# Moving the second batch's transposes and copies ahead of the convolution loop in a fused attention, routed-expert and gated-convolution kernel

## The chip, the core and the metric

The kernel runs on one core of a Trainium2 chip. The metric is the device time of one execution in microseconds (us); lower is better. The engines named below are PE (TensorE: matrix products; PEld is its weight load), DVE (VectorE), ACT (ScalarE), POOL (GpSimd) and SP (SyncE, which here issues DMAs). Each has its own list of instructions, in the order of the program, and semaphores tie the lists together.

## What is computed

The program chains three layers: an attention with cluster masks, a layer of routed experts, and a gated causal convolution. Only the third is touched here (B = 2 batches, S = 768 rows, D = 512 channels, 5 taps):

```
def _moe2_ref(x, w_val, conv_w, w_out):
    B, S, D = x.shape
    K = conv_w.shape[0]
    xp = np.concatenate([np.zeros((B, K - 1, D)), x], axis=1)
    gate_pre = np.zeros((B, S, D))
    for k in range(K):
        gate_pre += conv_w[k][None, None, :] * xp[:, k:k + S, :]
    gate = 1.0 / (1.0 + np.exp(-gate_pre))
    val = x @ w_val
    return gate * val @ w_out
```

## The kernel before

The last stage starts when the experts' output `x2d` is in DRAM. Both products are made to almost full float32 accuracy by splitting each operand into a high part (float32r) and the rest: `xh` and `xl` for x, `vh` and `vl` for w_val, `gh` and `gl` for the gated values, `oh_` and `ol` for w_out. A product is then high x high, low weight x high, and high weight x rest.

**Loads.** SP issues five loads of `x2d` into `xnat` (12 tiles of 128 rows: tile 0, tiles 1-2, 3-5, 6-8 and 9-11; L1075 to L1078). Between the fourth and the fifth it issues the two 1 MB loads of the output weights (L1080, through L293 and L294).

**Transposes.** `x2_tiles(b, t0, n, eng)` takes n tiles of batch b. PE transposes each into a PSUM tile `x2p` (4 transposes of 128x128 a tile, L1102). ACT rounds it into `xh` (L1106), `eng` copies it, unrounded, into `xf` (L1107); after every third tile DVE forms that half of `xl` = `xf` - `xh` (L1111, two instructions). Batch 1's six tiles all go through the two PSUM buffers of the pool `ps_x`, so a transpose of tile t waits until both copies of tile t-2 are done. For batch 0 the copies to `xf` are on DVE, and three of its tiles use the pool `ps_g`; for batch 1 they are on ACT.

**Channels.** A batch has four blocks d of 128 channels, and `order` lists the eight (b, d). For each, `conv0` (ACT, first tap), `conv_a` (DVE, a tap per instruction) and `conv_b` (ACT, the sigmoid) make the gate in `gt`; `value` makes 24 matmuls of 384 columns into a PSUM tile `vp` of the pool `ps_g` (three buffers): `value_hi` 8 for each half c of the rows, then `value_lo` 4 for each half. `value_out` copies `vp` to `vs` on ACT, which frees the buffer; `gated` multiplies on DVE and rounds on ACT into `gh`; `gated_rest` forms `gl` on DVE. `project(b, t)` makes 12 matmuls of 512 columns for one tile of the output, copies it on ACT and stores it.

**Order.** It is written out by hand: nothing moves instructions afterwards. Batch 0's tiles come first, then the value products of (0, 0) and (0, 1), then a loop over n = 1 to 7, in which each step does parts of the gate of `order[n]`, finishes `order[n - 1]`, copies out earlier value products (`evict`), and issues matmuls for later ones (`after[n]`: `value(0, 2)` at n = 1, `value(0, 3)` at n = 2, `value(1, 0)` and `value(1, 1)` at n = 3, `value(1, 2)`, `value(1, 3)` and the projections after). Batch 1's tiles are taken in pairs in steps 1, 2 and 3:

```
        for m in evict.get(n, ()):
            value_out(*order[m])
        if n < 4:
            x2_tiles(1, 2 * n - 2, 2, nc.scalar.copy)
        if n < 7:
            conv0(*order[n + 1])
        gated(*order[n - 1])
```

Of the kernel before, what the change touches and what calls it, by code (L numbers as in the profile page):

```python
# [8 lines left out]
F32 = mybir.dt.float32  # L9
# [4 lines left out]
ALU = mybir.AluOpType  # L14
# [18 lines left out]
def routed_attention_moe_kernel(  # L33
# [12 lines left out]
    nc = tc.nc  # L46
# [703 lines left out]
    for i in range(NI):  # L750
        g, qb, t, h = items[i]
# [334 lines left out]
    xh, xl, xf, gh, gl = ({} for _ in range(5))  # L1086

    def x2_tiles(b, t0, n, eng):
        if t0 == 0:
            xf[b] = ft.tile([128, 4, S + 4], F32, tag=f"xf{b}", name="xf")  # L1090
            nc.gpsimd.memset(xf[b][:, :, 0:4], 0.0)
            xh[b] = fx.tile([128, 4, S], F32R, tag="xh", name="xh")
            xl[b] = fx.tile([128, 4, S], F32R, tag="xl", name="xl")
        xps = []
        for t in range(t0, t0 + n):
            if b == 0 and 2 <= t < 5:
                xps.append(ps_g.tile([128, 2, 512], F32, tag="v", name="x2p")[:, 0, :].rearrange("p (d c) -> p d c", d=4))
            else:
                xps.append(ps_x.tile([128, 4, 128], F32, tag="x", name="x2p"))
        for i in range(n):  # L1100
            for d in range(4):
                nc.tensor.transpose(xps[i][:, d, :], xnat[:, 6 * b + t0 + i, 128 * d:128 * d + 128], ident)  # L1102
        for i in range(n):
            t = t0 + i
            ts = slice(128 * t, 128 * t + 128)
            nc.scalar.copy(xh[b][:, :, ts], xps[i])  # L1106
            eng(xf[b][:, :, 4 + 128 * t:132 + 128 * t], xps[i])  # L1107
            if t % 3 == 2:
                c0 = 128 * t - 256
                for d in range(0, 4, 2):  # L1110
                    nc.vector.tensor_tensor(  # L1111
                        xl[b][:, d:d + 2, c0:c0 + 384], xf[b][:, d:d + 2, 4 + c0:388 + c0],
                        xh[b][:, d:d + 2, c0:c0 + 384].bitcast(F32), op=ALU.subtract,
                    )

    G = {}

    def conv0(b, d):
        G[b, d] = fl.tile([128, S], F32, tag="gt", name="gt", bufs=3)
        nc.scalar.activation(G[b, d], xf[b][:, d, 0:S], AF.Copy, scale=convw_sb[:, d, 0:1])  # L1120

    def conv_a(b, d, ks):
        for k in ks:
            nc.vector.scalar_tensor_tensor(  # L1124
                G[b, d], xf[b][:, d, k:k + S], convw_sb[:, d, k:k + 1], G[b, d], op0=ALU.mult, op1=ALU.add
            )

    def conv_b(b, d):
        nc.scalar.activation(G[b, d], G[b, d], AF.Sigmoid)  # L1129
# [3 lines left out]
    def value_hi(b, d, c):  # L1133
        ds_, cs_ = slice(128 * d, 128 * d + 128), slice(384 * c, 384 * c + 384)
        if c == 0:
            V[b, d] = ps_g.tile([128, 2, 512], F32, tag="v", name="vp")
        for k in range(4):
            nc.tensor.matmul(V[b, d][:, c, :384], vh[:, k, ds_], xh[b][:, k, cs_], start=(k == 0), stop=False)  # L1138
            nc.tensor.matmul(V[b, d][:, c, :384], vl[:, k, ds_], xh[b][:, k, cs_], start=False, stop=False)  # L1139

    def value_lo(b, d, c):
        ds_, cs_ = slice(128 * d, 128 * d + 128), slice(384 * c, 384 * c + 384)
        for k in range(4):
            nc.tensor.matmul(V[b, d][:, c, :384], vh[:, k, ds_], xl[b][:, k, cs_], start=False, stop=(k == 3))  # L1144
# [6 lines left out]
    def value_out(b, d):  # L1151
        VS[b, d] = fl.tile([128, S], F32, tag="vs", name="vs", bufs=3)
        nc.scalar.copy(VS[b, d].rearrange("p (a c) -> p a c", a=2), V.pop((b, d))[:, :, :384])  # L1153

    def gated(b, d):
        if d == 0:
            gh[b] = fx.tile([128, 4, S], F32R, tag="xh", name="gh")
            gl[b] = fx.tile([128, 4, S], F32R, tag="xl", name="gl")
        gt = G.pop((b, d))
        nc.vector.tensor_tensor(gt, gt, VS.pop((b, d)), op=ALU.mult)  # L1160
        nc.scalar.copy(gh[b][:, d, :], gt)
        GT[b, d] = gt

    def gated_rest(b, d):
        nc.vector.tensor_tensor(  # L1165
            gl[b][:, d, :], GT.pop((b, d)), gh[b][:, d, :].bitcast(F32), op=ALU.subtract
        )
# [30 lines left out]
    for t in range(6):  # L1198
        x2_tiles(0, t, 1, nc.vector.tensor_copy)
# [11 lines left out]
    conv0(0, 0)  # L1211
    conv_a(0, 0, (1, 2, 3, 4))
    conv0(0, 1)
    for f in (value_hi, value_lo):
        for c in range(2):
            for d in range(2):
                f(0, d, c)
    for n in range(1, 8):
        conv_a(*order[n], (1, 2))
        conv_b(*order[n - 1])  # L1220
        for m in evict.get(n, ()):
            value_out(*order[m])
        if n < 4:
            x2_tiles(1, 2 * n - 2, 2, nc.scalar.copy)
        if n < 7:
            conv0(*order[n + 1])
        gated(*order[n - 1])
        conv_a(*order[n], (3,))
        gated_rest(*order[n - 1])
        conv_a(*order[n], (4,))  # L1230
        for f in after[n]:
            f()
# [56 lines left out]
```

## Time and profile before

| | us |
|---|---|
| median of 3 runs | 581.74 |
| lowest and highest of them | 581.27, 582.97 |
| the profiled execution, its own time | 581.82 |
| span of the profiled execution | 580.1 |
| last stage, from the first load issued to the end | 488.25 to 580.1 |

All times of rows are counted from the start of the span of one profiled execution. A timeline row gives start and duration of an instruction, or of several of one kind merged (x8), and in brackets how long the engine had been idle before it and what ended that. Matmuls overlap in the pipeline, so the step from one start to the next is what one costs, not its duration. PEclk is the clock granted to TensorE, 1.00 for 2.4 GHz and 0.50 for 1.2 GHz.

### The profile page before, as it was taken

What the parts mean: (1) busy time and instruction counts of PE and PEld (TensorE: products, weight loads), DVE (VectorE), ACT (ScalarE), POOL (GpSimd) and SP (SyncE); (2) the same over time, 40 slices, a digit from 0 to 9 for tenths busy, and PEclk for the clock granted to TensorE, in tenths of its full rate; (3) what the DMA queues carried; (4) which work ended last, traced back from release to release, by engine and by line L of the source; (5) the groups of instructions that cost most, each with busy time, mean ns of one, the idle gap of its engine ahead of it and who ended that gap; (6) DMA issues with size and microseconds to landing.
All of it is one profiled execution on the core that took longest, in us unless ns stands there. A gap on an engine that the chain in (4) does not pass through costs nothing. (4 is left out here: it accounts for less than half of the span.)

```text
span 580.1 us, 9383 instructions
## 1 busy us (share of the span) xinstructions
PE 550.8 (95%) x3485; PEld 442.6 (76%) x3485; DVE 386.5 (67%) x661; ACT 338.7 (58%) x611; POOL 114.6 (20%) x105
## 2 busy tenths in 40 slices
PE   7889999999999999997899999999999998978996
PEld 3756777776767776775788989989989884878885
DVE  5675767575878866467268769678687370887940
ACT  3676777777777686751255655656555352466532
POOL 4001010101030210303530440522504432000000
PEclk9899999999999999997999999999999999997999
DMA  6977777673747464102658778678678775700012
GB/s 147 267 170 237 153 245 157 206 157 96 164 144 156 159 137 141 40 35 105 217 181 311 238 255 297 217 281 282 218 279 281 290 262 188 294 0 2 36 73 108
DMA packets 33103, 104.82 MB, mean 181 GB/s; under 512 B 5713, under 2 KB 6225, under 8 KB 27936
## 3 DMA queue, kind: packets, MB, share of 16 engines
q1 hardware_dynamic: 28816, 97.31, 54.3%
q0 software_dynamic: 3280, 6.32, 2.9%
q8 instruction: 28, 0.46, 0.3%
q10 hardware_dynamic: 960, 0.58, 0.3%
q14 instruction: 19, 0.16, 0.1%
HBM read 63.45 MB, written 24.95 MB: 152 GB/s over the span
## 5 line engine op out<-in xcount | busy, mean ns | idle before, releaser
L620 DVE TENSOR_REDUCE mx<-s 128x1 f32<-128x768 f32 x96 | 91.6, 955 | 60.0 <-PE s L613 53.9
L321 DVE TENSOR_TENSOR wlo<-wraw,whi 128x1024 fp32r<-128x1024 f32 x66 | 89.9, 1364 | 22.8 <-ACT whi L320 22.3
L649 ACT COPY pt<-tp 128x384 f32<-128x384 f32 x148 | 66.0, 487 | 53.8 <-PE tp L644 53.7
L629 ACT ACTIVATE pexp<-s,mx 128x768 f32<-128x768 f32 x96 | 87.5, 912 | 7.6 <-DVE mx L620 5.5
L320 ACT CAST whi<-wraw 128x1024 fp32r<-128x1024 f32 x68 | 70.2, 1045 | 30.7 <-DMA wraw<-in_wq_dram 30.6
L644 PE MATMUL tp<-ident,pexp 128*128 128x128 f32 x576 | 81.4, 277 | 0.6 <-DVE pt L647 0.4
L644 PEld LDWEIGHTS tp<-ident,pexp 128*128 128x128 f32 x576 | 68.2, 142 | 8.2 <-ACT pt L649 3.4
L656 PE MATMUL pv<-pt,vt 128*64 128x384 f32 x360 | 67.8, 498 | 0.2 <-ACT ut L665 0.2
L609 PE MATMUL s<-st 128*128 128x384 f32 x188 | 57.3, 386 | 1.5 <-ACT pexp L629 1.5
L987 PE MATMUL yp<-whi,hhi 128*128 128x512 f32 x136 | 53.8, 395 | 0.0
L991 PE MATMUL yp<-whi,hlo 128*128 128x512 f32 x136 | 53.7, 395 | 0.0
L990 PE MATMUL yp<-wlo,hhi 128*128 128x512 f32 x136 | 53.7, 395 | 0.0
L613 PE MATMUL s<-st 80*128 80x384 f32 x188 | 49.1, 342 | 2.4 <-DMA st<-ohr 2.4
L964 ACT ACTIVATE hhi<-hps 128x512 fp32r<-128x512 f32 (+1 forms) x36 | 20.7, 576 | 51.4 <-PE hps L960 41.6
L965 DVE SCALAR_TENSOR_TENSOR hlo<-hps,hhi 128x512 fp32r<-128x512 f32 (+1 forms) x36 | 23.6, 656 | 31.0 <-ACT hhi L964 25.3
L960 PE MATMUL hps<-xhi,whi 128*128 128x256 f32 x256 | 41.9, 284 | 1.6 <-issue 0.9
L609 PEld LDWEIGHTS s<-st 128*128 128x128 f32 x188 | 28.6, 191 | 18.0 <-ACT pt L649 6.8
L960 PE MATMUL hps<-xlo,whi 128*128 128x256 f32 x256 | 41.2, 280 | 0.6 <-issue 0.4
L960 PE MATMUL hps<-xhi,wlo 128*128 128x256 f32 x256 | 40.7, 279 | 0.0
L656 PEld LDWEIGHTS pv<-pt,vt 128*64 128x64 f32 x360 | 21.9, 136 | 24.1 <-issue 23.7
L339 POOL TENSOR_TENSOR xx<-xkq,xx 128x768 fp32r<-128x768 f32 x8 | 14.6, 1822 | 120.8 <-ACT xx L333 102.6
L238 POOL TENSOR_TENSOR wspace<-wspace 128x512 f32<-128x512 f32 x8 | 14.2, 1781 | 120.8 <-ACT wspace L234 110.3
(225 smaller groups left out, 983.6 us busy)
## 6 DMA issues: line engine op xcount, KB each, us to landing
wraw<-in_wq_dram SPq DMA_DIRECT2D x34, 1024.0 KB, 5.1
st<-xx SPq DMA_DIRECT2D x48, 384.0 KB, 6.8
xkq<-in_kq_dram SPq DMA_DIRECT2D x15, 384.0 KB, 4.4
xslots<-padrow SPq DMA_DIRECT2D x8, 514.0 KB, 7.8
wspace<-in_wd_dram SPq DMA_DIRECT2D x8, 512.0 KB, 5.3
xs<-xslots SPq DMA_DIRECT2D x7, 514.0 KB, 5.8
vt<-in_v_dram SPq DMA_DIRECT2D x8, 384.0 KB, 3.4
out_dram<-os SPq DMA_DIRECT2D x11, 256.0 KB, 2.0
```

Of the source, the lines that this page charges most:

```text
L320: nc.scalar.copy(hi[:, c], t[:, c])
L321: (lo_eng or nc.vector).tensor_tensor(lo[:, c], t[:, c], hi[:, c].bitcast(F32), op=ALU.subtract)
L609: nc.tensor.matmul(ps[:, n, :384], st[:, 1, q0:q0 + 128], st[:, 0, 384 * n:384 * n + 384], start=True, stop=False)
L620: nc.vector.tensor_reduce(mx, ps[:, :, :384], axis=AX.XY, op=ALU.max, negate=True)
L629: nc.scalar.activation(pt, ps[:, :, :384], AF.Exp, bias=mx[:, 0:1], accum_out=Zt[i // 6][:, t, h:h + 1])
L644: nc.tensor.transpose(tp[:, k, :], p[:, 128 * kt:128 * kt + 128], ident)
L649: nc.scalar.copy(dst, tp)
L656: nc.tensor.matmul(PVs[u][64 * h:64 * h + 64, :], Vt[g][:, kt, h, :], PT[u, h][:, kt, :], start=(kt == 0), stop=(kt == NQT - 1), skip_grou ...
L960: nc.tensor.matmul(hp[:, fi, :w], a[:, d, fs], c[:, d, :w], start=(n + d == 0), stop=(n + d == 5))
L987: nc.tensor.matmul(yp[t], hhi[:, fa, ts], whv[:, f, :], start=(q == 0 and f == 0), stop=False)
L990: nc.tensor.matmul(yp[t], hhi[:, fa, ts], wlv[:, f, :], start=False, stop=False)
L991: nc.tensor.matmul(yp[t], hlo[:, fa, ts], whv[:, f, :], start=False, stop=(q == 1 and f == 3))
```

## The change

Batch 1's six tiles are no longer taken in the loop. Two of them come after the first eight matmuls of `value(0, 0)`, two after its next eight, two after the sixteen of `value_hi(0, 1, ...)`; only then come the sixteen of `value_lo`. The subtractions for `xl` of batch 1 are taken out of `x2_tiles` into `x2_rest` and stay in the loop, at n = 1 and n = 2. The numbers of instructions are the same on every engine.

```
@@ x2_tiles
-            if t % 3 == 2:
-                c0 = 128 * t - 256
-                for d in range(0, 4, 2):
-                    nc.vector.tensor_tensor(
-                        xl[b][:, d:d + 2, c0:c0 + 384], xf[b][:, d:d + 2, 4 + c0:388 + c0],
-                        xh[b][:, d:d + 2, c0:c0 + 384].bitcast(F32), op=ALU.subtract,
-                    )
+            if b == 0 and t % 3 == 2:
+                x2_rest(b, t // 3)
+
+    def x2_rest(b, half):
+        c0 = 384 * half
+        for d in range(0, 4, 2):
+            nc.vector.tensor_tensor(
+                xl[b][:, d:d + 2, c0:c0 + 384], xf[b][:, d:d + 2, 4 + c0:388 + c0],
+                xh[b][:, d:d + 2, c0:c0 + 384].bitcast(F32), op=ALU.subtract,
+            )
@@ after conv0(0, 1)
-    for f in (value_hi, value_lo):
-        for c in range(2):
-            for d in range(2):
-                f(0, d, c)
+    for c in range(2):
+        value_hi(0, 0, c)
+        x2_tiles(1, 2 * c, 2, nc.scalar.copy)
+    for c in range(2):
+        value_hi(0, 1, c)
+    x2_tiles(1, 4, 2, nc.scalar.copy)
+    for c in range(2):
+        for d in range(2):
+            value_lo(0, d, c)
     for n in range(1, 8):
...
-        if n < 4:
-            x2_tiles(1, 2 * n - 2, 2, nc.scalar.copy)
+        if n in (1, 2):
+            x2_rest(1, n - 1)
```

On PE, after the last of `value(0, 0)`'s first eight matmuls, the program before went on to `value(0, 1)`; `vp_5662` is that one's PSUM tile, `vp_5653` that of `value(0, 0)`, and the bracket names the engine whose semaphore is waited for:

```order
L1139 MATMUL vp_5653<-xh_5597,wlo_5344 128x384
L1138 MATMUL vp_5662<-xh_5597,whi_5343 128x384 [waits DVE_49]
...
L1138 MATMUL vp_5653<-xh_5597,whi_5343 128x384 [waits Activation_49]
...
L1144 MATMUL vp_5653<-xl_5598,whi_5343 128x384 x4
```

The changed program has, at the same place, transposes of batch 1's first four tiles (`x2p_5666`, `x2p_5667`, `x2p_5688`, `x2p_5689`), with the second eight matmuls of `value(0, 0)` between them and `value(0, 1)` (`vp_5702`) behind; DMAHW5 and DMAHW0 are the loads of tiles 6-8 and 9-11:

```order
L1102 MATMUL x2p_5666<-ident_140,x2nat_5575 128x128 [waits DMAHW5_49]
...
L1102 MATMUL x2p_5667<-ident_140,x2nat_5575 128x128 [waits DVE_49]
...
L1141 MATMUL vp_5653<-xh_5597,whi_5343 128x384 [waits Activation_49]
...
L1102 MATMUL x2p_5688<-ident_140,x2nat_5575 128x128 [waits PE_49,Activation_49]
L1102 MATMUL x2p_5688<-ident_140,x2nat_5575 128x128 x3
L1102 MATMUL x2p_5689<-ident_140,x2nat_5575 128x128 [waits DMAHW0_49,PE_49,Activation_49]
L1102 MATMUL x2p_5689<-ident_140,x2nat_5575 128x128 x3
L1141 MATMUL vp_5702<-xh_5597,whi_5343 128x384
```

So the transposes of the fourth of these tiles, which need the last load, now stand ahead of all of `value(0, 1)` and of every `value_lo`.

On ACT, from the two `conv0` on, the difference begins so (- is before; the pair of copies, xh and xf, stands six times in the new order):

```order
-L1120 ACTIVATE gt<-xf,convw_sb 128x768 x2
-L1129 ACTIVATE gt<-gt 128x768
-L1153 COPY vs<-vp 128x768 x2
-L1106 CAST xh<-x2p 128x4x128
+L1123 ACTIVATE gt<-xf,convw_sb 128x768 x2
+L1106 CAST xh<-x2p 128x4x128
+L1107 COPY xf<-x2p 128x4x128
```

The first sigmoid and the first two copies of `vp` to `vs`, which stood right behind the two `conv0`, now stand behind all twelve copies of batch 1. On DVE the two `xl` pairs of batch 1 move earlier, the first from behind `gl` of (0, 0) to ahead of the first multiply.

## Rows read from the trace of the kernel before

**Rows 1.** The page: busy time of PE, its share of the span, instructions.
```profile
PE 550.8 (95%) x3485; PEld 442.6 (76%) x3485; DVE 386.5 (67%) x661; ACT 338.7 (58%) x611; POOL 114.6 (20%) x105
```

**Rows 2.** Stretches of 10 us: busy time by engine, then PEclk, DMA share, GB/s.
```profile
520.00:530.00 10.00, 5.07 (x20) 5.07 (x21) 8.40 (x10) 5.26 (x8) 0.00 (x0) 0.66 0.01 2
560.00:570.00 10.00, 10.00 (x45) 8.04 (x44) 0.36 (x1) 0.00 (x0) 0.00 (x0) 1.00 0.07 26
```

**Rows 3.** Timeline of PE, from the stall to the first projection.
```profile
519.10 0.34 PE L1139 MATMUL vp<-xh,wlo 128*128 128x384 f32 x1
524.93 0.69 PE L1138 MATMUL vp<-xh,whi 128*128 128x384 f32 x1 [5.49 <-ACT xh L1106]
...
529.45 0.33 PE L1138 MATMUL vp<-xh,whi 128*128 128x384 f32 x1
...
533.61 0.33 PE L1138 MATMUL vp<-xh,whi 128*128 128x384 f32 x1
...
541.93 0.40 PE L1180 MATMUL op<-whi,gh 128*128 128x512 f32 x1
```

**Rows 4.** Timeline of ACT, ahead of the end of that stall.
```profile
521.88 0.84 ACT L1129 ACTIVATE gt<-gt 128x768 f32<-128x768 f32 x1 [1.95 <-DVE gt L1124]
```

**Rows 5.** Timeline of PE, the first value products.
```profile
498.54 0.34 PE L1139 MATMUL vp<-xh,wlo 128*128 128x384 f32 x1
...
503.28 2.94 PE L1144 MATMUL vp<-xl,whi 128*128 128x384 f32 x16
506.06 1.03 PE L1102 MATMUL x2p<-ident,x2nat 128*128 128x128 f32 x8
506.85 0.42 PE L1138 MATMUL vp<-xh,whi 128*128 128x384 f32 x1
```

**Rows 6.** Timeline of DVE, start of the stage, a later xl, the end.
```profile
498.26 1.88 DVE L1107 COPY xf<-x2p 128x512 f32<-128x512 f32 x3
...
501.91 6.16 DVE L1124 SCALAR_TENSOR_TENSOR gt<-xf,convw_sb,gt 128x768 f32<-128x768 f32 x6
...
516.37 1.83 DVE L1111 TENSOR_TENSOR xl<-xf,xh 128x768 fp32r<-128x768 f32 x2 [0.59 <-ACT xf L1107]
...
559.40 0.96 DVE L1165 TENSOR_TENSOR gl<-gt,gh 128x768 fp32r<-128x768 f32 x1 [0.91 <-ACT gh L1161]
```

**Rows 7.** Timeline of ACT: the two conv0, then a pair of copies.
```profile
500.23 1.77 ACT L1120 ACTIVATE gt<-xf,convw_sb 128x768 f32<-128x768 f32 x2 [2.04 <-DVE xf L1107]
...
508.25 0.60 ACT L1106 CAST xh<-x2p 128x512 fp32r<-128x512 f32 x1
508.73 0.61 ACT L1107 COPY xf<-x2p 128x512 f32<-128x512 f32 x1
```

**Rows 8.** Tile x2nat, issues from 492.5 to 493.2 (tiles 9-11).
```profile
L1076 SPq DMA_DIRECT2D x2nat<-x2d x1: 475/475/475, 492.6 to 492.6; - x1
...
DMA to landing us min/median/max: 13.8/13.8/13.8
```

**Rows 9.** Stretches of 1 us, columns as in rows 2.
```profile
504.00:505.00 1.00, 1.00 (x7) 1.00 (x6) 0.98 (x1) 0.00 (x0) 0.00 (x0) 1.00 0.27 94
...
528.00:529.00 1.00, 1.00 (x6) 1.00 (x5) 1.00 (x2) 0.84 (x1) 0.00 (x0) 0.76 0.00 0
```

**Rows 10.** Timeline of PE, ahead of the stage's first transposes.
```profile
490.06 2.78 PE L104 MATMUL spin<-onesb 128*128 128x512 bf16 x8 [2.14 <-ACT warm L1085]
```

**Rows 11.** Timeline of PE, a wait early in the attention.
```profile
44.55 0.59 PE L613 MATMUL s<-st 80*128 80x384 f32 x2 [2.44 <-DMA st<-ohr]
```

**Rows 12.** Other stretches, columns as in rows 2.
```profile
43.79:47.20 3.41, 2.49 (x17) 2.17 (x18) 2.03 (x3) 1.37 (x3) 0.00 (x0) 1.00 0.67 169
...
265.65:269.07 3.42, 2.87 (x16) 1.49 (x17) 2.58 (x20) 0.33 (x1) 0.71 (x1) 0.50 0.00 0
269.07:272.48 3.41, 3.41 (x13) 2.17 (x11) 2.91 (x14) 0.00 (x0) 2.22 (x3) 0.50 0.43 159
...
490.93:494.35 3.42, 3.42 (x13) 2.22 (x12) 0.00 (x1) 0.59 (x1) 0.00 (x0) 0.50 0.92 298
```

## Prediction

> **What bounds the kernel now.** Read the page first: PE is busy for 95% of the span [rows 1], so only a stretch in which PE isn't can give much back. The stretches of 10 us show one in the last stage: from 520 to 530 PE is busy for 5.07 us at a mean granted clock of 0.66, while from 560 to 570 it is full at 1.00 [rows 2]. PE's timeline gives the place: `value(1, 0)`'s first half of `value_hi` starts at 519.10 for the last time, then PE sits idle for 5.49 us until ACT has rounded `xh` of batch 1's last tiles, at 524.93. The sixteen matmuls after that take 529.45 - 524.93 = 4.52 us, where 24 take 533.61 - 529.45 = 4.16 us, 0.173 each, at the full clock, or 2.77 for sixteen. So the stall costs 5.49, and the half clock after it 1.75 [rows 3]. From there to the first projection at 541.93 and on to the end PE is fed without a gap, so what moves 541.93 moves the end. Why was `xh` late? ACT stands in line behind the sigmoid of step 3, which had itself waited 1.95 us for DVE's taps [rows 4]: the tiles are paced by the gate's chain in the loop, though nothing in the tiles needs it.
>
> **The change, part by part.** The counts of instructions are equal on every engine, and no DMA is moved. So the sum is a walk along PE from the point where the orders part, after the matmul that starts at 498.54 [rows 5], to the first projection.
>
> *Transposes.* Eight take 506.85 - 506.06 = 0.79 us [rows 5]. The first four of batch 1 start at 498.7. The next four need the PSUM buffer of batch 0's last tile, which DVE leaves at 500.14 (498.26 + 1.88) [rows 6]. Then come eight matmuls (1.4 us, to 502.0). The third four need both copies of the first tile from ACT, which is in its two `conv0` until 502.0; a copy costs 0.48 (508.73 - 508.25), so they start at 503.0 [rows 7].
>
> *The last load.* The fourth four need tile 9, and that is in the load issued at 492.61, which lands 13.8 us later, at 506.4 [rows 8]. This is the term that decides: before, these transposes came so late that the load was never waited for. Now all that is behind them on PE, the sixteen matmuls of `value_hi(0, 1)`, the last eight transposes and the sixteen of `value_lo`, waits for 506.4, and the waits of 1.0 us each before it are absorbed in it. How sure is 506.4? From 504 to 505 the queue moves only 94 GB/s [rows 9]: a few late packets hold the load, so it could land up to 1.0 us sooner; later than 506.4 nothing here points to.
>
> *From 506.4 at the full clock.* 4 transposes 0.40, 16 matmuls 2.77, 8 transposes 0.79, 16 matmuls 2.77: `value(0, 2)` starts at 513.2, where before it started at 506.85 [rows 5], 6.3 us later than before. But sixteen fewer transposes and no stall lie ahead: six products of 4.16 bring PE to the first projection at 538.2, against 541.93. That is 3.7 us gained, if nothing else holds PE.
>
> *The clock.* Between 502.0 and 506.4 PE now works for 0.4 us only. Twice the trace shows what such a pause does. A wait of 2.14 us ahead of 490.06 [rows 10] was followed by the half clock from 490.93 to 494.35; a wait of 2.44 us at 42.1 to 44.55 [rows 11] was not: the next stretch is at 1.00 [rows 12]. The new pause is longer than both, 4.4 us with a crumb of work in it, so I take the fall. Its price: after 524.93 the half clock lasted some 3.6 us of work (0.76 in 528 to 529 [rows 9]) and cost 1.75, so 0.49 per us; from 265.65 to 272.48 it lasted 6.8 us with PE busy in most of it [rows 12], which here would cost 3.3. The nearest row is the spell after 524.93, but there the clock had fallen well before work resumed; here it falls near the resumption, as at 490.93. I take 4.5 us, 2.2 us of cost; the ends are 1.75 and 3.3. The Trainium skill ("TensorE: Matmul & The Clock Gate", section "Why this matters for your kernels") warns against long idle gaps of PE between bursts of matmuls, since the clock then falls back to half. By that rule the fall is certain and the sum 580.3; the row at 44.55 shows a gap that passed, and by it the sum would be 578.1.
>
> *ACT and DVE.* Twelve copies (5.8 us) now stand ahead of the first sigmoid and the first two `value_out`. With the half clock the last transposes end at 512.6, their four copies at 514.5, the sigmoid (0.84 [rows 4]) at 515.3 and the first `vs` at 516. DVE, through its taps at 508.1 (501.91 + 6.16) and the first `xl` pair at 509.9 (1.83) [rows 6], idles 6 us for it. That costs nothing as long as `gl` of (0, 3) is there for the first projection at 540.4 (538.2 + 2.2): from 516 to it DVE has 21 instructions of at most 1.03 (6.16 / 6) and the other `xl` pair [rows 6], 23.5 us, so 539.5 at the latest. The cover is 0.9 us; once it is gone, each us late is a us of the end. At the far end `gl` of (1, 3) was there at 560.4 [rows 6], while PE came to it only behind six projections of 12 matmuls and 9 each of five more: 117 matmuls at 10 / 45 = 0.22 us [rows 2] after 541.93, at about 568. That leaves over 7 us.
>
> *Sum.* 581.82 (the profiled execution; the median is 581.74, so nothing to correct) - 3.7 + 2.2 = 580.3.
>
> **The rivals.**
> 1. *Stall traded for a load and a fall of the clock* (the forecast): 580.3; with the cost of the clock between 1.75 and 3.3 it is 579.9 to 581.4, and with the load up to 1 us sooner (part of which the clock takes back) 579.0.
> 2. *The clock holds.* For it: 44.55 [rows 11], and transposes are put into the pause. Against it: two waits in a row. 581.82 - 3.7 = 578.1, with a sooner load 577.2.
> 3. *The gate's chain becomes the bound, slower than before.* DVE starts its multiplies at 516 and no longer behind its taps at 508.1. If each of the four steps to `gl` of (0, 3) also waits for `gh` as the last one did before (0.91 [rows 6]), it comes at 539.5 + 3.6 = 543.1, and the projections 1.2 us later than before: 583.0. It decides from 541.9 on, so 2.4 us of such waits are enough. Against it: the 1.03 per instruction is an upper bound, and ACT has fewer copies in the loop, so `gh` is less often late.
> 4. *The change doesn't bring PE forward*: the half clock holds for 7.5 us (3.7 / 0.49) or more after 506.4, or `value(1, 0)` waits again, now for the second `xl` pair, which DVE reaches 8 us late. Six instructions and that pair behind 516 it is ready at 524.0; PE wants it behind `value(0, 2)`, `value(0, 3)` and sixteen matmuls, at 515.4 + 8.3 + 2.8 = 526.5, which speaks against it. 581.8.
>
> **How the numbers follow.** Chances: 0.60, 0.22, 0.10, 0.08. A measurement of this kernel can hardly tell 0.3% from no change (the runs spread from 581.27 to 582.97), so faster means under 580.0, slower over 583.5. The forecast lies just inside "same"; its range is 579.0 to 581.4, of which I give two fifths to the faster side. Faster: 0.22 + 0.25 = 0.47. Same: 0.35 from the first, half of the third and half of the fourth, 0.44. Slower: the rest of these two, 0.09. The range from 577.6 to 582.2 holds nearly all of cases 1 and 2 and half of case 4.
>
> **What the profile of the changed kernel would show.** PE idle ahead of the fourth group of transposes until about 506.4, put down to the load of `x2nat`; no idle time of several us ahead of `value(1, 0)`; a stretch with half clock beginning between 503 and 507 and no second one from 520 to 530; the first projection at about 540.4 and the last matmul at about 574. DVE idle for about 6 us ahead of its first multiply. I'd be wrong if the load lands by 504 (then PE hardly waits), if PEclk stays at 1.00, or if PE waits for DVE's `gl` ahead of the projections.

## The result, and the profile after

The changed kernel takes **573.56 us** (median of 4 runs, 572.93 to 573.86), the kernel before 581.94 beside it (4 runs, 581.27 to 582.97): a ratio of 0.984, with a 95% interval of 0.981 to 0.987. The forecast was 580.3, with a range from 577.6 to 582.2. So the change gains 8.4 us where 1.4 were forecast, and the median lies below the range. Its profiled execution took 573.4 us, with a span of 571.7.

The page's line of busy time, against [rows 1]:

```profile
PE 546.9 (96%) x3485; PEld 439.8 (77%) x3485; DVE 386.9 (68%) x661; ACT 338.9 (59%) x611; POOL 115.1 (20%) x105
```

PE has 3.9 us less busy time, half clock included, and the span is 8.4 us shorter. Stretches of the change, columns as in [rows 2]:

```profile
500.75:501.75 1.00, 0.13 (x1) 0.16 (x2) 0.96 (x2) 0.70 (x2) 0.00 (x0) 1.00 0.02 6
501.75:502.75 1.00, 1.00 (x8) 1.00 (x8) 1.00 (x2) 0.46 (x1) 0.00 (x0) 1.00 0.00 0
502.75:503.75 1.00, 1.00 (x8) 1.00 (x7) 0.96 (x2) 0.61 (x2) 0.00 (x0) 1.00 0.07 16
520.00:530.00 10.00, 10.00 (x59) 10.00 (x58) 9.93 (x11) 6.96 (x9) 0.00 (x0) 1.00 0.01 2
```

The hole of [rows 2] is gone: from 520 to 530 PE is full at 1.00. There is a new one between 500.75 and 501.75, and behind it PEclk is still 1.00. PE's timeline shows what PE waits for now, in the transposes of batch 1 and nowhere behind them; the last row is the first projection:

```profile
496.73 0.66 PE L1102 MATMUL x2p<-ident,x2nat 128*128 128x128 f32 x4 [0.98 <-DVE xf L1107]
499.55 0.66 PE L1102 MATMUL x2p<-ident,x2nat 128*128 128x128 f32 x4 [0.76 <-ACT xf L1107]
501.62 0.63 PE L1102 MATMUL x2p<-ident,x2nat 128*128 128x128 f32 x4 [1.41 <-DMA x2nat<-x2d]
...
504.89 1.03 PE L1102 MATMUL x2p<-ident,x2nat 128*128 128x128 f32 x8
505.68 3.02 PE L1147 MATMUL vp<-xl,whi 128*128 128x384 f32 x16
...
533.50 0.40 PE L1183 MATMUL op<-whi,gh 128*128 128x512 f32 x1
```

These are the three waits of the prediction's walk, in its order: DVE's copy of batch 0's last tile, ACT's copies of the first tile, the last load. Against [rows 3], 5.49 us of stall became 3.15 us in three waits. SP's timeline shows where the stage begins, in the change and then in the kernel before:

```profile
484.75 3.19 SPq L1076 DMA_DIRECT2D x2nat<-x2d  x4
```

```profile
488.25 3.02 SPq L1076 DMA_DIRECT2D x2nat<-x2d  x4
```

This is the second thing to see: the changed kernel is 3.5 us ahead **before the stage that was changed begins**. On every engine the two programs have the same instructions up to that stage. Most of the lead arises between 285 and 302 us, in the experts. A stretch there, of before and then of the change, columns as in [rows 2]:

```profile
285.00:300.00 15.00, 13.66 (x110) 12.77 (x109) 8.21 (x12) 7.61 (x12) 8.93 (x9) 1.00 0.40 138
```

```profile
285.00:300.00 15.00, 15.00 (x131) 15.00 (x130) 10.60 (x15) 8.74 (x13) 8.88 (x8) 1.00 0.48 145
```

PE is idle for 1.34 us in the one and for nothing in the other. PE's timeline from one group of the experts' transposes to the next, of before and then of the change; "issue" is time in which an engine waited for nothing that the profile shows:

```profile
287.28 1.04 PE L922 MATMUL xp<-ident,xs 128*128 128x128 f32 x8
...
294.66 0.49 PE L960 MATMUL hps<-xhi,whi 128*128 128x256 f32 x2 [0.43 <-issue]
...
296.11 0.36 PE L960 MATMUL hps<-xlo,whi 128*128 128x256 f32 x1 [0.45 <-issue]
...
297.54 0.72 PE L960 MATMUL hps<-xhi,whi 128*128 128x256 f32 x4 [0.45 <-issue]
...
301.86 1.03 PE L922 MATMUL xp<-ident,xs 128*128 128x128 f32 x8
```

```profile
286.38 1.03 PE L922 MATMUL xp<-ident,xs 128*128 128x128 f32 x8
...
298.57 1.04 PE L922 MATMUL xp<-ident,xs 128*128 128x128 f32 x8
```

At the first group the change is 0.90 us ahead, at the second 3.29. The gaps don't belong to one program: after_again, the changed kernel once more, has five of them, 2.51 us in all, and they are in nine of the thirteen profiles below. The four without them (the change, after_third, late_rest and spread) are the four whose last stage begins earliest. What causes them the profiles don't show.

So in these two profiles 8.4 us of span are 3.5 ahead of the stage and 4.9 in it (from 580.1 - 488.25 = 91.9 to 571.7 - 484.75 = 87.0). The experiments ask whether both belong to the change, and why the stage gained 4.9 where the walk had 3.7 and the clock was to take back 2.2.

### The profile page after: what moved, and what is told of

It is laid out like the page before. It is cut to its first block, busy times and chain, and to the rows that moved or that the text cites. A ratio compares the mean times of both kernels' runs of the same rounds, so it can differ in the third digit from the quotient of the medians.

```text
span 571.7 us, 9383 instructions
## 1 busy us (share of the span) xinstructions
PE 546.9 (96%) x3485; PEld 439.8 (77%) x3485; DVE 386.9 (68%) x661; ACT 338.9 (59%) x611; POOL 115.1 (20%) x105
## 5 line engine op out<-in xcount | busy, mean ns | idle before, releaser
L609 PEld LDWEIGHTS s<-st 128*128 128x128 f32 x188 | 28.6, 191 | 18.2 <-ACT pt L649 6.8
```

The costliest lines, as they stand in the source:

```text
L609: nc.tensor.matmul(ps[:, n, :384], st[:, 1, q0:q0 + 128], st[:, 0, 384 * n:384 * n + 384], start=True, stop=False)
```

## The experiments

Each profile is cut at three rows: the first load issued (the stage's start), the start of the fourth group of moved transposes (the end of the pause for the last load), the end of the span. Lengths in us; the column is blank where the kernel has no such group:

| kernel | stage starts at | fourth group, after that | from there to the end | stage |
|---|---|---|---|---|
| before | 488.25 | | | 91.9 |
| before_again | 493.88 | | | 92.1 |
| before_spins | 489.68 | | | 90.3 |
| the change | 484.75 | 16.87 | 70.1 | 87.0 |
| after_again | 487.81 | 17.40 | 70.1 | 87.5 |
| after_third | 485.29 | 17.87 | 70.0 | 87.9 |
| load_first | 489.31 | 15.88 | 70.1 | 86.0 |
| load_later | 490.85 | 20.40 | 72.4 | 92.8 |
| late_spins | 488.24 | 19.81 | 70.0 | 89.8 |
| late_rest | 487.14 | 17.01 | 77.0 | 94.0 |
| late_rest_again | 489.06 | 16.82 | 76.9 | 93.7 |
| spread_only | 489.74 | (other order) | | 84.2 |
| spread | 484.24 | (other order) | | 83.2 |

### Both kernels again (before_again, after_again, after_third)

No edit. Theory A is that the change shortens the last stage by 4.7 to 4.9 us and the rest of the 8.4 is chance ahead of it; the rival, that all 8.4 belong to the change.

> The kernel before, unchanged, once more. The profile showed 8.4 us gained, of which only 4.9 lie in the last stage (91.8 us before, 86.9 after, from its first load to the end); 3.5 lie ahead of it, between 285 and 300 us, where the two programs hold the same instructions. Theory A (the 3.5 us belong to this execution or chip, not to the change): the stage again takes 91.8 within 0.5, and its start may fall anywhere from 484 to 489. Theory B (the 3.5 us belong to the change): the stage starts at 488.2 within 0.5 and the time is 581.8.

> The changed kernel, unchanged, once more, beside the kernel before on the same chip. Theory A (the 3.5 us ahead of the stage are chance): the stage takes 86.9 again, its start wanders, and the ratio to the kernel before lies near 1 - 4.9 / 581.8 = 0.992. Theory B (they come with the change): start 484.7 again and a ratio of 0.985.

> A third profile of the changed kernel; it leaves nothing out. Theory A (the change shortens the last stage by 4.7 to 4.9 us, the rest of the first difference is wander ahead of the stage): the stage takes 86.5 to 88 us, wherever between 484 and 494 us it begins, and the granted clock is 1.00 behind the pause for the last load. Rival (the clock holds in that pause by chance): half clock behind it this time, and a stage of 88.5 to 89.5 us.

Beside a kernel before at 583.98 us (29 runs, 580.55 to 588.55), before_again took 584.86 (10 runs; ratio 1.001, 0.998 to 1.004) and after_again 578.25 (12 runs; ratio **0.990, 0.988 to 0.993**). Stages that begin at 493.88 and 487.81 are as long as in the first pair, within 0.6, and neither start is the one that the rival needs. But 493.88 is also later than the 484 to 489 that theory A allowed. PE's timeline of after_again, and a stretch behind its wait with the busy time of PE alone, PEclk, DMA share and GB/s:

```profile
505.21 0.63 PE L1102 MATMUL x2p<-ident,x2nat 128*128 128x128 f32 x4 [1.84 <-DMA x2nat<-x2d]
```

```profile
505.81:506.81 1.00, 1.00 (x8) 1.00 0.00 0
```

The third profile of the change (574.96 us, one run, beside one of 585.41 before) shows the latest load of the three, 2.19 us of wait for it, and still PEclk 1.00 behind it. PE's timeline, then a stretch, columns as in the last one:

```profile
503.16 0.63 PE L1102 MATMUL x2p<-ident,x2nat 128*128 128x128 f32 x4 [2.19 <-DMA x2nat<-x2d]
```

```profile
503.29:504.29 1.00, 1.00 (x8) 1.00 0.00 0
```

The stage takes 91.9 and 92.1 us before, 87.0, 87.5 and 87.9 after: the change is worth 3.9 to 5.2 us there, 4.5 in the mean, which is 0.992 of 584 and lies in the second interval; 0.984 doesn't. The first ratio of 0.984 is thus not explained by the stage alone. Its start wanders from 484.2 to 493.9 over these profiles, all with the same instructions ahead of it. The three with the order of before begin at 490.6 in the mean and the ten with the new order at 487.6, with ranges that overlap; whether some of that belongs to the change isn't settled. The times hint that it does. In each of the seven measurements of several runs with the new order, the gain in the median over the kernel before beside it is larger than the gain in the stage (against 92.0, the mean of the two), by 1.0 to 3.3 us; in before_spins it is larger by 0.2. This is an estimate, since each stage was read from one profile, and it names no cause. So theory A is right about the stage, but that all the rest is chance is not shown.

In the table the column behind the pause is the finding: 70.0 to 70.1 three times. What differs among the three stages is when the last load lands, nothing else.

### The stall filled with dummy work (before_spins)

To the kernel before, 30 products that nobody reads are added in `value(1, 0)`, between the halves of `value_hi`, where PE was idle for 5.49 us:

```
+SPINS = 30
...
+    def value_spun(b, d):
+        value_hi(b, d, 0)
+        for _ in range(SPINS):
+            nc.tensor.matmul(V[b, d][:, 1, :384], onesb, ..., start=True, stop=True)
+        value_hi(b, d, 1)
...
-        3: [lambda: value(1, 0), lambda: value(1, 1)],
+        3: [lambda: value_spun(1, 0), lambda: value(1, 1)],
```

> The kernel before with thirty matmuls on constants (0.163 us each, 4.9 in all) put into the stall between the two halves of value(1, 0), so that PE is not idle there; they are overwritten. Prices the half clock by itself. Theory: the clock stays at 1.00 in 520 to 530 and the sixteen matmuls behind the stall take 2.8 instead of 4.5 us, so the stage is 1.75 shorter, 90.1. Rival (the half clock cost nothing because DVE set the pace behind it): 91.8.

Measured: 582.14 us (12 runs; ratio 0.997, 0.995 to 1.000). PE's timeline with the dummies and the wait that is left, then a stretch behind it, columns as in [rows 2]:

```profile
520.82 5.05 PE L1155 MATMUL vp<-onesb 128*128 128x384 bf16 x30
526.47 0.44 PE L1139 MATMUL vp<-xh,whi 128*128 128x384 f32 x1 [0.60 <-ACT xh L1107]
```

```profile
527.00:528.00 1.00, 1.00 (x8) 1.00 (x7) 1.00 (x2) 0.94 (x1) 0.00 (x0) 1.00 0.06 16
```

The clock stays at 1.00 and the stage is 1.5 to 1.8 us shorter (90.3 against 91.9 and 92.1), though it does more work: the half clock's 1.75 of the prediction is a real and separate loss.

### The last load sooner and later (load_first, load_later, late_spins)

load_first issues all five loads of x2 ahead of the 2 MB of output weights:

```
-        if t0 == 6:
-            w_dma(LAST + 2)
+    w_dma(LAST + 2)
```

load_later puts two more loads of 256 KB ahead of the fifth:

```
         if t0 == 6:
             w_dma(LAST + 2)
+            for _ in range(2):
+                extra = fl.tile([128, 512], F32, tag="os", name="extra")
+                nc.sync.dma_start(extra, wq[0, :, 0:512])
```

> The changed kernel with the last load of x2 issued ahead of the two 1 MB loads of output weights. Theory (the last load is what PE waits for last among the moved transposes, 1.41 us in the changed kernel): PE's wait for x2nat ahead of the fourth group disappears, the first projection comes 1.3 us sooner in the stage, stage 85.6. Rival (the copies on ACT or the gate's chain take the wait's place): PE waits for ACT there instead and the stage stays at 86.9.

> The changed kernel with 512 KB of other data (two loads that nothing uses) put into SP's queue ahead of the last load of x2, so that it lands some 1.3 us later and PE's pause ahead of the fourth group of transposes grows from 3.0 to about 4.3 us, the length that the prediction had worked out. Theory (a pause of that length brings the half clock, as the prediction had it; it failed only because the load came sooner): half clock from about the end of the pause, stage 86.9 to 87.5 + 1.3 + 2 = 90.4. Rival (the transposes inside the pause are enough, the clock holds there too): stage 88.5.

load_first: 576.94 us (6 runs; ratio 0.987, 0.982 to 0.991, beside after_again). In its timeline of PE no wait for the load is left in the moved transposes, and waits for the copies come out from behind it:

```profile
501.40 0.66 PE L1101 MATMUL x2p<-ident,x2nat 128*128 128x128 f32 x4 [1.53 <-DVE xf L1106]
504.21 0.66 PE L1101 MATMUL x2p<-ident,x2nat 128*128 128x128 f32 x4 [0.76 <-ACT xf L1106]
505.19 0.66 PE L1101 MATMUL x2p<-ident,x2nat 128*128 128x128 f32 x4 [0.32 <-ACT xf L1106]
```

The fourth group starts 1.0 to 2.0 us sooner than in the three profiles of the change, and the stage is 1.0 to 1.9 us shorter: the theory's 1.3 is inside, and the rival's copies take back 0.32.

load_later: 581.24 us (10 runs; ratio 0.997, 0.993 to 1.001, beside 582.45): nearly all of the change's gain is lost. The pause in PE's timeline, then stretches around its end with PE's busy time, PEclk, DMA share and GB/s:

```profile
511.25 1.08 PE L1105 MATMUL x2p<-ident,x2nat 128*128 128x128 f32 x4 [4.91 <-DMA x2nat<-x2d]
```

```profile
507.85:508.85 1.00, 0.00 (x0) 1.00 0.50 193
508.85:509.85 1.00, 0.00 (x0) 0.89 0.25 90
...
511.85:512.85 1.00, 1.00 (x6) 0.50 0.00 0
```

The load was to land 1.3 us later and landed 2.5 to 3.5 later; but here the clock did fall, inside a wait of 4.91 us, and the way from the pause to the end is 72.4 us long, 2.3 more than in the change. Is that the clock? late_spins is load_later with 28 dummy products in the pause, between the third and the fourth group of transposes:

```
         for i in range(n):
+            if (b, t0, i) == (1, 2, 1):
+                V[0, 1] = ps_g.tile([128, 2, 512], F32, tag="v", name="vp")
+                for _ in range(28):
+                    nc.tensor.matmul(V[0, 1][:, 0, :384], onesb, ..., start=True, stop=True)
             for d in range(4):
...
-        if c == 0:
+        if c == 0 and (b, d) not in V:
```

> The kernel with the later last load, and 28 dummy products (384 columns each, into a value tile of which nothing is read yet) between the third and the fourth group of moved transposes, where TensorE waited 4.91 us and the clock then fell for 6.8 us. Theory C (the 5.8 us that the later load cost are 3.6 us of lateness and 2.2 us of half clock): the granted clock stays at 1.00 behind the pause and the last stage takes about 90.5 us, against 92.74 us without the dummies and 86.9 to 87.5 us for the changed kernel. Rival (all of the 5.8 us is lateness, the half clock is hidden): the clock holds and the stage still takes 92 to 93 us.

PE's timeline with the dummies, then a stretch behind them, columns as in the last one:

```profile
503.50 4.71 PE L1107 MATMUL vp<-onesb 128*128 128x384 bf16 x28
508.05 0.60 PE L1111 MATMUL x2p<-ident,x2nat 128*128 128x128 f32 x4
```

```profile
508.24:509.24 1.00, 1.00 (x9) 1.00 0.00 0
```

Here the dummies end the pause, not the load, for which PE doesn't wait at all. The clock holds, the fourth group starts 19.81 us into the stage and the rest takes 70.0 us again: a stage of 89.8, 0.7 below what theory C had and 3.0 below load_later's, of which 0.6 is the sooner group and 2.4 the clock. The rival is out.

### The subtractions for xl left one step later (late_rest, late_rest_again)

```
-        if n in (1, 2):
-            x2_rest(1, n - 1)
+        if n in (2, 3):
+            x2_rest(1, n - 2)
```

> The changed kernel with the two xl pairs of batch 1 one step later, at n = 2 and 3, where the kernel before had them. Theory (moving the transposes alone would leave the second pair too late for value(1, 0), so the earlier place of the subtractions is part of the gain): DVE ends the second pair about 5.7 us later, PE waits some 2 us for it inside value(1, 0), stage 89. Rival (PE has enough other work): stage 87.

> A second profile of the kernel whose subtractions for xl are left one step later in the convolution loop; it leaves nothing out. The first had a stage of 93.95 us, with half clock behind the pause in the moved transposes and again behind the wait for xl. Theory (the wait for xl, about 3 us, and the fall of the clock behind it belong to the place of the subtractions; the fall in the transposes is chance): the wait for xl is 2.5 to 3.5 us again, the clock falls behind it again, the clock holds in the transposes, and the stage takes 91 to 92.5 us. Rival (the fall in the transposes belongs to this kernel too): both falls again, 93.5 to 94.5 us.

late_rest took 582.91 us (10 runs; ratio 1.000, 0.995 to 1.004): this alone undoes the change, and at 94.0 the stage is 5 us over the theory's 89. Both profiles have the same two losses. PE's timeline of the first, and stretches behind its two waits, columns as above:

```profile
504.15 0.63 PE L1102 MATMUL x2p<-ident,x2nat 128*128 128x128 f32 x4 [1.67 <-DMA x2nat<-x2d]
...
527.55 0.61 PE L1147 MATMUL vp<-xl,whi 128*128 128x384 f32 x2 [2.95 <-DVE xl L1114]
```

```profile
505.14:506.14 1.00, 1.00 (x5) 0.50 0.00 0
...
529.00:530.00 1.00, 1.00 (x5) 0.50 0.06 16
```

The same two views of the second profile:

```profile
503.80 0.66 PE L1102 MATMUL x2p<-ident,x2nat 128*128 128x128 f32 x4 [0.76 <-ACT xf L1107]
505.88 0.76 PE L1102 MATMUL x2p<-ident,x2nat 128*128 128x128 f32 x4 [1.42 <-DMA x2nat<-x2d]
...
529.29 0.62 PE L1147 MATMUL vp<-xl,whi 128*128 128x384 f32 x2 [2.98 <-DVE xl L1114]
```

```profile
507.00:508.00 1.00, 1.00 (x4) 0.50 0.00 0
...
531.00:532.00 1.00, 1.00 (x5) 0.50 0.06 16
```

In the first, the wait for xl costs 3.7 us (eight matmuls take 5.12 us, from 523.75 to 528.87, instead of 8 x 0.173), the fall behind it 1.6 (sixteen from 528.87 to 533.21) and the fall behind the pause 1.6 (sixteen from 504.53, and the next group at 508.97; 4.44 us where after_third has 2.89). That makes the 6.9 us by which the last part exceeds 70.0. Without the last of the three, 5.3 us would be left, still more than the 4.5 that the change gains. The second profile was to have only one fall and had both, so the theory that the first fall was chance lost its test. But on PE no instruction ahead of that fall differs from the change, where the clock held three times, behind 0.76 and 1.41 us of wait in the first profile and 0.75 and 2.19 in the third. In late_rest it fell behind 0.26 and 1.67, in late_rest_again behind 0.76 and 1.42. What decides it isn't in these rows, and it stays open.

### A better place (spread, spread_only)

The pairs of tiles are put further apart, so that no group waits for copies; spread is that on top of load_first, spread_only on the change itself:

```
     for c in range(2):
         value_hi(0, 0, c)
-        x2_tiles(1, 2 * c, 2, nc.scalar.copy)
+    x2_tiles(1, 0, 2, nc.scalar.copy)
     for c in range(2):
         value_hi(0, 1, c)
-    x2_tiles(1, 4, 2, nc.scalar.copy)
-    for c in range(2):
-        for d in range(2):
-            value_lo(0, d, c)
+    x2_tiles(1, 2, 2, nc.scalar.copy)
+    for d in range(2):
+        value_lo(0, d, 0)
+    x2_tiles(1, 4, 2, nc.scalar.copy)
+    for d in range(2):
+        value_lo(0, d, 1)
```

> The load order of the run before with the last load first, and the moved transposes placed later among the matmuls: both halves of value_hi(0, 0), a pair of tiles, both of value_hi(0, 1), a pair, half of value_lo, a pair, the other half. Theory (each of PE's waits among the moved transposes, 2.6 us in that run, is for a buffer or a load that is there a little later, so other matmuls can cover it): waits under 0.5 us, first projection 2.3 us sooner, stage 83.5. Rival (gl of (0, 3), the gate's chain, becomes the bound): PE waits for DVE ahead of the first projection, stage about 85.5.

> The changed kernel with the same later placing of the transposes, the loads in their old order. Tells the placing from the load: by the theory PE comes to the fourth group about 15.8 us into the stage and waits under 1 us for the load; stage 84.2. Rival (the load holds PE as before, whatever stands ahead of it): stage 87.

spread: **571.10 us** (6 runs; ratio 0.982, 0.977 to 0.988, beside 582.45), spread_only 573.52 (4 runs; 0.984, 0.977 to 0.991). In spread's timeline of PE the groups of batch 1 are eights without a wait, and PE waits for nothing from there to the end (the last row is the first projection); spread_only, in the fence behind it, has one wait there:

```profile
495.85 1.13 PE L1101 MATMUL x2p<-ident,x2nat 128*128 128x128 f32 x8
...
499.59 1.18 PE L1101 MATMUL x2p<-ident,x2nat 128*128 128x128 f32 x8
...
502.00 1.03 PE L1101 MATMUL x2p<-ident,x2nat 128*128 128x128 f32 x8
...
529.25 0.40 PE L1182 MATMUL op<-whi,gh 128*128 128x512 f32 x1
```

```profile
506.63 0.63 PE L1102 MATMUL x2p<-ident,x2nat 128*128 128x128 f32 x4 [0.81 <-DMA x2nat<-x2d]
```

Stages of 83.2 and 84.2 us: the order of the groups is worth about 3.3 us on the change's 87.5, the loads' order 1.0 more. Both are faster than the kernel before. Against the change itself spread's stage is 3.8 to 4.7 us shorter; the ratios, each against other runs of the kernel before, meet at the edge (0.977 to 0.988 and after_again's 0.988 to 0.993).

## Why the prediction was wrong, step by step

**The stall and its price: right.** The 5.49 us in `value(1, 0)` are gone, and before_spins gives the half clock behind them 1.5 to 1.8 us, against 1.75.

**The walk along PE: right.** From the last load's landing at 506.4 to the projections at 538.2 it had 31.8 us, with the 38.2 behind them 70.0; three profiles show 70.0 to 70.1. The two waits that it put at 1.0 us each came as 0.98 and 0.76 in the first profile, in that order. The change also lives by the earlier subtractions, as rival 4 said in the other direction: put back one step, they hold `value(1, 0)` for 3 us.

**The clock: the step that failed.** "I take the fall", with 0.60 for it. In none of the three profiles of the change did the clock fall in the pause; rival 2, with 0.22, was the right one, and its walk of 3.7 us stands. That is in part luck: with late_rest's two, whose order on PE is the same up to there, the clock held in three profiles of five. Its price was right: 2.2 forecast, 2.3 to 2.4 in load_later and late_spins, which do what the forecast described. The wrong part was the pause. It was put at 4.4 us, because the load was put at 506.4 and the third group at 503.0. From the end of the eight matmuls to the fourth group it was 2.8, 3.3 and 3.6 us, and the waits for the load in it were 1.41, 1.84 and 2.19 us. The third group came where it was put (14.80 to 15.02 us into the stage, against 503.0 - 488.25 = 14.75); what shortened the pause was the load. A fall after 2.14 us and none after 2.44 [rows 10, 11] had already said that a pause of this size doesn't settle it, and late_rest says so again. The Trainium skill ("TensorE: Matmul & The Clock Gate", section "Why this matters for your kernels") warns of idle gaps between bursts of matmuls; the gap of 4.91 us agrees with it, while for the shorter ones the rows here have both answers.

**The last load: a size that was off.** The text allowed "up to 1.0 us sooner" than 18.2 us into the stage [rows 8]; in the change the group behind it started at 16.87, 17.40 and 17.87, in before_again and late_rest_again the load landed at 16.6 and 16.7. The trace that the estimate was read from had the latest of those landings. In the first profile that is 1.3 us, and 3.7 + 1.3 = 5.0 against 91.9 - 87.0 = 4.9.

**The sum's base: the largest part of the miss, and never priced.** "Nothing to correct" took the profiled execution as a fixed base; three runs lay within 1.7 us. Twenty-nine runs of the same kernel spread over 8 us. Between the predicted end of the span (580.1 - 1.5 = 578.6) and the measured one (571.7) lie 6.9 us: about 2.2 of clock, 1.3 of load, and 3.5 that were there before the stage began. Without these 3.5 the time would have been 577.1, next to rival 2's 577.2 with the sooner load. Why PE has gaps at 285 to 302 us in some profiles and none in others was not tried, and the cause stays open.

**The gate's chain (rival 3): didn't happen.** DVE's timeline, its first multiply and the last `gl` that the first projection wants:

```profile
509.05 0.96 DVE L1163 TENSOR_TENSOR gt<-gt,vs 128x768 f32<-128x768 f32 x1 [2.70 <-ACT vs L1156]
...
530.09 0.96 DVE L1168 TENSOR_TENSOR gl<-gt,gh 128x768 fp32r<-128x768 f32 x1
```

DVE idled 2.70 us, not 6 (the 6 included the half clock: in late_rest it idled 6.23), and `gl` ended at 531.05, 2.45 us ahead of the projection at 533.50, against 0.9 forecast. In spread, whose first projection is 3.7 us sooner in its stage (45.0 against 48.75), PE still didn't wait for it, with 1.1 us left.

## What to carry to other kernels

Price a moved instruction by what it is moved ahead of: here the gain was the old stall, less what the new place waits for (the load, the copies), and putting the groups where both were there or nearly gave another 3.3 us (spread_only). The consumers' other inputs must move along (the `xl` subtractions), or the gain is gone. Before a sum of single us is trusted, cut several profiles of the same kernel at the first instruction that the change touches, since what lies ahead can move more than the change does.

## What was not expected of the hardware

The start of the last stage wandered from 484.2 to 493.9 us over thirteen profiles whose instructions ahead of it are the same; the eight that are known to be of one chip have both ends. And with the same order of PE's instructions and waits of the same size, the granted clock stayed at 1.00 in the change (0.76 and 1.41 us) and fell to 0.50 in late_rest_again (0.76 and 1.42).
